# Reordering the transposes, the stores and the pooling of a pooled-attention and MLP kernel

## The chip, the core and the metric

The kernel runs on one core of a Trainium2 chip. The core has five engines that work side by side, each on its own queue of instructions in order: TensorE (PE; its weight loads are shown apart as PEld), VectorE (DVE), ScalarE (ACT), GpSimd (POOL) and SyncE (SP). SP computes nothing; it issues transfers and DMA transposes. GpSimd issues transfers too, between its own computations. The metric is the device time of the whole program in microseconds (us), as a median over runs.

## The reference

Inputs are q, k and v of shape (8 batches, 8 heads, 576 positions, 64), and two weight matrices. For each batch and head, k and v are averaged over groups of 8 neighbouring positions, so 72 pooled keys and values remain. Each of the 576 queries attends to the 72 pooled keys. The result, 4608 tokens of 512 values, goes through a two-layer block:

```python
k_p = k.reshape(B, H, Sp, pool, D).mean(axis=3)
v_p = v.reshape(B, H, Sp, pool, D).mean(axis=3)
scores = scale * np.matmul(q, k_p.transpose(0, 1, 3, 2))
attn = softmax(scores)          # written out in the reference
x = np.matmul(attn, v_p)        # then heads side by side: (4608, 512)
h = x @ w_in                    # (4608, 2048)
g = h * np.cos(h)
out = g @ w_out                 # (4608, 512)
```

## The kernel before, in words

**Two loops in one.** The MLP works on nine tiles of 512 tokens, the loop over t from 0 to 8. The attention works on eight batches of 576 tokens, and is woven into the same loop: while tile t is in the MLP, the attention of batch b = t + 1 is made. Tile t + 1 takes the last tokens of batch t and the first 448 - 64 t tokens of batch t + 1. Attention for a batch goes in chunks: u0, u1, u2 and u3 of 128 positions each, and a rest ur of 64 positions, which is made one tile later.

**One tile.** First come the up matmuls (`up_mm`, L342) with x transposed in `xT` as the moving operand. ScalarE takes a cosine of each result (L352) and VectorE multiplies (L356) into `g_sb`. Then come seven products with w_out (`down_products`, L420). Seven products take the place of eight because sums and differences of the halves of `g_sb` and of the weights are formed first: `put_g(k, i)` (L386) writes g1 to g4 from `g_sb`, each in two halves i. Some of these combinations run between the up results (at n = 3, 4 and 5), the others at the start of the products. The products use two PSUM banks in turn (A and Bb, the obanks), and after each product a VectorE read, `reads[0]` to `reads[6]` (L434, L436), takes the bank's content into SBUF. The next product in the same bank cannot start before that read. `reads[1]` frees the bank for `product(3)`. The reads write the results into `o_two`, of which there are two buffers; they are written to HBM by `rows_out` (L456), eight stores of 128 KB per tile, all issued by SP.

**The attention in a tile.** Between the products, TensorE computes scores (L222) for u0, u1 and u2, ScalarE takes the exponential (L229), and `values_rows` multiplies with the pooled v (L284). VectorE divides by the sums (`inv_rows`, L287, and `x_rows`, L289). SP then transposes `x_rows` into `xT` with a DMA transpose (L293). u3 and ur follow between the later products. The next tile's up matmuls read these columns of `xT`.

**What prepares a batch.** GpSimd loads k, q and v of the next batch (`load_kv`, L114, and `load_q`, L95) and sums groups of eight positions in `pool_add`: first sums over four pairs (L151, four instructions), then L153 (two), and for k two instructions at L156 that write `kp2`, for v one at L159 that writes `vz`. All go through one buffer `half_sums`. SP transposes pooled k into `kk` (`k_transpose`, L182) and q into `qT` (`q_transpose`, L195).

**What sets the order.** The order is written out by hand. Each engine runs its instructions in the order of the program text; waits come from the data that an instruction reads and writes. The text issues `q_transpose(b)` after the first pair of up results (n == 0) and `k_transpose(b)` after the third (n == 2), but the eight stores of the tile before stand ahead of both on SP's queue, after the transposes of u3. At the end of a tile's text GpSimd copies one element of `kk` into `gate` (L688). This copy does nothing but wait for the k transpose; the three loads of the next batch are queued behind it, and the pooling behind the loads.

Of the kernel before, what the change touches and what calls it, by code (L numbers as in the profile page):

```python
# [20 lines left out]
def kernel(  # L21
# [64 lines left out]

    staged = {}

    def even_view(src, b, j0=0, j1=KCH):
        return src[b, 2 * j0:2 * j1].rearrange("(j a) (p t) d -> (a p) j (t d)", a=2, t=ROW)
# [25 lines left out]
    def load_q(b):  # L118
        q_tile(b)
        load_even(staged["q", b], b, q)  # L120
# [21 lines left out]
            for r in range(2):  # L142
                copy(out=dst[half[r], pj0:pj1, a, 0:Sp], in_=ps[half[a]])

    def pool_add(b, which):

        st = staged.pop((which, b))
        x, s = st, half_sums
        add = nc.gpsimd.tensor_tensor
        for h in range(0, H, 2):  # L150
            add(out=s[:, h:h + 2], in0=x[:, h:h + 2, 0:4, :], in1=x[:, h:h + 2, 4:8, :], op=ADD)  # L151
        for h in range(0, H, 4):
            add(out=s[:, h:h + 4, 0:2, :], in0=s[:, h:h + 4, 0:2, :], in1=s[:, h:h + 4, 2:4, :], op=ADD)  # L153
        if which == "k":
            for slot in range(2):
                add(out=kp2[b % 2][:Sp, :, slot, :], in0=s[:, :, 0, :], in1=s[:, :, 1, :], op=ADD)  # L156
        else:
            s = s.rearrange("p (j a) t d -> p j a t d", a=2)
            add(out=v_part(b), in0=s[..., 0, :], in1=s[..., 1, :], op=ADD)  # L159
# [21 lines left out]
    def k_transpose(b):  # L181
        nc.sync.dma_start_transpose(out=kk[b % 2], in_=kp2[b % 2].rearrange("p h s d -> p (h s d)"))  # L182
# [10 lines left out]
    def q_transpose(b):  # L193
        qT_tile(b)
        nc.sync.dma_start_transpose(out=att["qT", b], in_=q_flat(b))  # L195
# [196 lines left out]
    def down_products(t):  # L392
# [36 lines left out]
        def each(out, bank, other=None, m=slice(0, HM), tk=None):  # L429

            for p in range(2) if apart else (slice(0, 2),):
                ps = bank[p] if apart else obanks[1 if bank is A else 0].rearrange("p (a m) -> p a m", a=2)
                if other is None:
                    (nc.scalar.copy if t >= B - 1 else nc.vector.tensor_copy)(out=out[:, p, m], in_=ps)  # L434
                else:
                    nc.vector.tensor_tensor(out=out[:, p, m], in0=ps, in1=other[:, p], op=ADD)  # L436
                if apart and tk is not None:
                    rows_out(t, tk, out, (p,), m, (nc.sync, nc.scalar))
# [4 lines left out]
            lambda: each(v16, A, p1),  # L443
            lambda: each(q15, Bb, p1),
            lambda: each(o2, A, q15, m2, 1),
            lambda: (each(o1, Bb, v16, m2, 0), apart or rows_out(t, 0, o1)),
            lambda: (each(o2, A, p1, m1, 1), apart or rows_out(t, 1, o2)),
        ]
        return [mms[i * 2 * HF:(i + 1) * 2 * HF] for i in range(7)], reads

    def rows_out(t, tk, o, ps=(0, 1), m=slice(0, d_model), queues=(nc.sync, nc.sync)):
        rows_of = out.rearrange("(b p t) m -> b t p m", b=B, t=ROW)
        for p in ps:
            for i, rows in enumerate(half):
                b_, pos = divmod((t * TILE + tk * HT + p * 128) // 64 + i, ROW)
                queues[i].dma_start(out=rows_of[b_, ORDER[pos], :, m], in_=o[rows, p, m])  # L456
# [93 lines left out]
    for t in range(NT):  # L550
# [5 lines left out]
        for n, fp in enumerate(up_order(t)):  # L556
            up_mm(t, fp, 2 if n < 2 else 0)
            between = ()
            if t == 0:
                if fp == 4:  # L560
                    puts = pool_k_mm(1, obanks[0], 0, 2), pool_k_mm(1, obanks[1], 2, 4)
                elif fp in (5, 6):
                    g0 = 9 * (fp - 5)
                    puts = q_transpose_mm(1, obanks[0], g0, g0 + 5), q_transpose_mm(1, obanks[1], g0 + 5, g0 + 9)
                if fp in (4, 5, 6):
                    puts[0](vec)
                    between = ((puts[1], act),)
            up_g(t, fp, between)
            if 0 < t and 3 <= n < 6:
                put_gs(*[(k, 0) for k in (((3,), (1,), ()) if t == 1 else ((1, 2), (3,), (4,)))[n - 3]])  # L570
            if 0 < t and b < B:
                if n == 0:
                    q_transpose(b)
                elif n == 2:
                    k_transpose(b)
        mms = [(ms, fc) for ms in range(4) for fc in range(FFCH)]
        if t == 0:
            mms = [(ms, fc) for hm in range(2) for cg in (0, 2, 1, 3) for ms in range(2 * hm, 2 * hm + 2)
# [36 lines left out]
        else:  # L615
# [32 lines left out]
                put_g(2, 0)  # L648
            put_gs((1, 1), (2, 1))
            reads[0]()  # L650
            put_g(3, 1)
            reads[1]()
            if t == 1:
                put_g(4, 0)
            if steady:
                values_rows(*u0)
            product(2)
            reads[2]()
            muls()
            if steady:  # L660
                values_rows(*u1)
                values_rows(*u2)
# [20 lines left out]
            reads[6]()  # L683
        if t < B:
            sin_tables()
        if 0 < t and b + 1 < B:

            nc.gpsimd.tensor_copy(out=gate, in_=kk[b % 2][0:1, 0, 0:1])  # L688
        if b + 1 < B:
            load_kv(b + 1, "k", k)  # L690
            load_q(b + 1)
            load_kv(b + 1, "v", v)
            if t == 0:
                put_weights(0, nc.gpsimd, (3, 2, 4))
                put_weights(1, nc.gpsimd, (1,))
            pool_add(b + 1, "k")
            pool_add(b + 1, "v")
# [1 line left out]
_INS = ['q', 'k', 'v', 'moe_w_in', 'moe_w_out']  # L699
_OUTS = [((4608, 512), 'float32')]  # L700
# [25 lines left out]
```

The softmax here doesn't subtract the row's maximum and nothing guards it: scores larger than these inputs give would overflow.

## Time and profile before

| What | Value |
|---|---|
| median of 3 runs | 292.55 us (292.11 to 293.8) |
| the profiled execution | 290.39 us |
| its span, first to last instruction | 288.6 us |
| TensorE matmuls busy | 275.1 us (95%) |
| VectorE busy | 217.5 us (75%) |
| ScalarE busy | 164.2 us (57%) |
| GpSimd busy | 149.7 us (52%) |
| TensorE clock granted | full in all slices |

The span is the part of the execution in which instructions of the program run. Line numbers (L342) are those of the kernel before. An answer about one stretch of the span has a line with the stretch, its length, and then busy time and number of instructions for TensorE, its weight loads, VectorE, ScalarE and GpSimd, followed by the granted clock, the mean share of the 16 DMA engines and GB/s. In a list of waits, a line says which engine and line waited, for what, how long in total, how often, and the longest. In a timeline, a line has the start, the length, the engine, the line of the kernel, the operation, output and inputs with shapes, the count, and in brackets the idle time before it and what ended that. For a DMA, the time to landing runs from its issue to the moment its data are known to have arrived.

### The profile page before, as it was taken

The numbers are of one execution on the slowest core, as the hardware profiler recorded it, in microseconds if no ns is written. First come the engines' busy times: TensorE is split into PE (matmuls) and PEld (weight loads), VectorE is DVE, ScalarE is ACT, GpSimd is POOL, SyncE is SP. The second block draws the span as 40 slices with busy tenths as digits, with TensorE's granted clock in tenths as the row PEclk, the third lists the DMA queues.
The fourth block names the chain that finished last, engine by engine and source line by source line (L and its number), as shares of the span: only waits on it lengthen the run. The fifth ranks groups of instructions, "written<-read, shape, count | busy, mean of one in ns | idle before, by whom it ended". The sixth has DMA issues, their size and how long they took to land.

```text
span 288.6 us, 5827 instructions
## 1 busy us (share of the span) xinstructions
PE 275.1 (95%) x2338; PEld 175.9 (61%) x2360; DVE 217.5 (75%) x314; ACT 164.2 (57%) x193; POOL 149.7 (52%) x145
## 2 busy tenths in 40 slices
PE   7889999999979999999799999999999999999994
PEld 2545554447854696468645884488448854884583
DVE  6458747799947995799549966996699669856972
ACT  3786798368147735773556655665557456436600
POOL 8563079996698359933995299529930000000000
PEclk9999999999999999999999999999999999999999
DMA  7999999554998699769977998699680243006014
GB/s 161 200 207 206 206 205 216 120 99 53 184 119 172 89 179 99 153 107 169 138 159 104 166 134 143 127 149 137 127 160 2 55 98 68 0 9 138 2 36 109
DMA packets 57545, 36.12 MB, mean 125 GB/s; under 512 B 35248, under 2 KB 53168, under 8 KB 57520
## 3 DMA queue, kind: packets, MB, share of 16 engines
q0 software_dynamic: 19744, 18.07, 39.9%
q1 hardware_dynamic: 37136, 17.18, 36.2%
q10 hardware_dynamic: 640, 0.52, 0.8%
q8 instruction: 18, 0.29, 0.4%
q14 instruction: 7, 0.06, 0.1%
HBM read 36.70 MB, written 9.44 MB: 160 GB/s over the span
## 4 chain that ended last, share of the span: by engine, by line
PE 61%; DVE 8%; DMA 3%; ACT 2%; issue 1%; DVEq 0%
PE obank L420 27%; PE bank L342 25%; DVE g_sb L356 4%; PE obank L342 3%; DMA xT<-x_rows 3%; PE bank L222 2%; DVE g L386 2%; PE bank L420 2%; PE bank L284 2%; ACT cos L352 1%; DVE o_two L436 1%; PE bank L257 1%; ACT ex L229 0%; DVE xT L268 0%; ACT inv L263 0%
## 5 line engine op out<-in xcount | busy, mean ns | idle before, releaser
L342 PE MATMUL bank<-xT,w_in_sb 128*128 128x512 bf16 x495 | 113.0, 379 | 4.1 <-DMA xT<-x_rows 1.6
L352 ACT ACTIVATE cos<-bank,half_pi 128x1024 f32<-128x1024 f32 x64 | 70.3, 1113 | 60.5 <-PE bank L342 59.9
L356 DVE TENSOR_TENSOR g_sb<-bank,cos 128x1024 bf16<-128x1024 f32 x64 | 77.1, 1221 | 29.2 <-ACT cos L352 29.2
L342 PEld LDWEIGHTS <-w_in_sb 128*128 128x128 bf16 x576 | 55.8, 98 | 70.1 <-DMA xT<-x_rows 3.6
L151 POOL TENSOR_TENSOR half_sums<-kv_st 72x512 f32<-72x512 bf16 x48 | 56.1, 1195 | 26.7 <-DMA kv_st<-in_k_dram 26.3
L229 ACT ACTIVATE ex<-bank 72x1024 bf16<-72x1024 f32 (+1 forms) x40 | 35.0, 928 | 34.5 <-PE bank L222 34.4
L420 PEld LDWEIGHTS <-g 128*128 128x128 bf16 x512 | 47.9, 98 | 6.1 <-issue 0.3
L420 PE MATMUL obank<-w,g 128*128 128x256 bf16 x368 | 42.6, 272 | 0.2 <-DVE p_sb L434 0.2
L420 PEld LDWEIGHTS <-g_sb 128*128 128x128 bf16 x384 | 36.6, 98 | 7.8 <-DVE g_sb L356 1.3
L153 POOL TENSOR_TENSOR half_sums<-half_sums 72x512 f32<-72x512 f32 x24 | 30.8, 1305 | 0.0
L420 PE MATMUL obank<-w_out_sb,g_sb 128*128 128x256 bf16 x240 | 29.2, 273 | 0.5 <-DVE g_sb L356 0.5
L386 DVE TENSOR_TENSOR g<-g_sb 128x1024 bf16<-128x1024 bf16 x32 | 24.3, 760 | 0.5
L289 DVE TENSOR_TENSOR x_rows<-bank,inv_rows 128x512 bf16<-128x512 f32 x24 | 16.6, 692 | 0.8
L268 DVE TENSOR_TENSOR xT<-bank,inv 64x256 bf16<-64x256 f32 x14 | 5.9, 422 | 14.6 <-ACT inv L264 14.6
L156 POOL TENSOR_TENSOR kp<-half_sums 72x512 bf16<-72x512 f32 x12 | 15.7, 1329 | 0.5
L420 PE MATMUL obank<-w_out_sb,g 128*128 128x256 bf16 x112 | 15.6, 273 | 0.0
L420 PE MATMUL obank<-w,g_sb 128*128 128x256 bf16 x128 | 15.3, 273 | 0.0
L342 PE MATMUL obank<-xT,w_in_sb 128*128 128x512 bf16 x64 | 15.1, 379 | 0.0
L359 PE MATMUL obank<-w_out_sb,g_sb 128*128 128x512 bf16 x61 | 14.7, 379 | 0.4 <-issue 0.3
L386 DVE TENSOR_TENSOR g<-g_sb,g 128x1024 bf16<-128x1024 bf16 x16 | 12.9, 809 | 0.0
L222 PE MATMUL bank<-qT,kk 64*72 64x128 bf16 (+2 forms) x288 | 12.5, 221 | 0.1
L320 ACT ACT_TABLE_LOAD x9 | 11.5, 1283 | 0.9 <-PEq L710 0.7
(102 smaller groups left out, 262.9 us busy)
## 6 DMA issues: line engine op xcount, KB each, us to landing
out_dram<-o_two SPq DMA_DIRECT2D x64, 128.0 KB, 2.4
kv_st<-in_v_dram POOLq DMA_DIRECT2D x8, 576.0 KB, 14.4
kv_st<-in_k_dram POOLq DMA_DIRECT2D x7, 576.0 KB, 7.7
q_b<-in_q_dram POOLq DMA_DIRECT2D x6, 576.0 KB, 10.2
w_in_sb<-in_moe_w_in_dram POOLq DMA_DIRECT2D x4, 512.0 KB, 13.5
w_out_sb<-in_moe_w_out_dram POOLq DMA_DIRECT2D x4, 512.0 KB, 18.3
q_b<-in_q_dram POOLq DMA_DIRECT2D x4, 288.0 KB, 12.4
g_sb<-in_k_dram SPq DMA_DIRECT2D x1, 576.0 KB, 3.5
```

The costliest lines, as they stand in the source:

```text
L151: add(out=s[:, h:h + 2], in0=x[:, h:h + 2, 0:4, :], in1=x[:, h:h + 2, 4:8, :], op=ADD)
L153: add(out=s[:, h:h + 4, 0:2, :], in0=s[:, h:h + 4, 0:2, :], in1=s[:, h:h + 4, 2:4, :], op=ADD)
L156: add(out=kp2[b % 2][:Sp, :, slot, :], in0=s[:, :, 0, :], in1=s[:, :, 1, :], op=ADD)
L222: nc.tensor.matmul(pair[:Sp, bank, c:c + n].rearrange("p (g n) -> p g n", n=64), lhsT=kk[b % 2][half[r], h0 + i, 0:Sp], rhs=att["qT", b][h ...
L229: nc.scalar.activation(out=ex[:, 0:nh * n].rearrange("p (a n) -> p a n", a=2), in_=pair[:Sp, :, 0:nh * n // 2], func=ACTF.Exp, scale=scale ...
L289: nc.vector.tensor_tensor(out=x[0:n].rearrange("p (j a d) -> p j a d", j=KCH, a=2), in0=ps[0:n, :, 0:2 * (D + 2)].rearrange("p j (a w) -> ...
L342: nc.tensor.matmul(h[j] if h is obanks else h[:, j, :], lhsT=w_in_sb[fc // 4][:, ki, (fc % 4) * 128:(fc % 4 + 1) * 128], rhs=xT[:, ki, t * ...
L352: nc.scalar.activation(out=c, in_=ps, func=ACTF.Sin, bias=half_pi[:, :1])
L356: nc.vector.tensor_mul(out=o, in0=ps, in1=c)
L359: nc.tensor.matmul(o, lhsT=g_sb[:, fc, ms * 128:(ms + 1) * 128], rhs=w_out_sb[fc // 4][:, fc % 4, :], start=(fc == 0), stop=(fc == FFCH - 1))
L386: nc.vector.tensor_tensor(out=out[:, f0:f1], in0=x, in1=y, op=op)
L420: mms.append(lambda bank=bank, first=first, g=g, w=w, fc=fc, p=p: nc.tensor.matmul(bank[p], lhsT=g(fc, p), rhs=w(fc), start=(first and fc ...
```

## The change

The change moves work on four queues, and changes no computation.

- On SP, both transposes of the batch are issued at n == 0, k before q. The eight stores of a tile are put in a list, and issued in the next tile at n == 2, after these transposes.
- The pooling is cut in two functions, `pool_first` (the four first sums) and `pool_rest`. At the end of tile t, GpSimd does k's first sums, k's rest and v's first sums. The rest of v follows in the next tile's text, at n == 2.
- The gate on `kk` and the three loads of the next batch move from the end of the text of tile t to n == 2 of the same tile, behind v's rest (in t = 1, the k load goes ahead of v's rest).
- In place of the old gate, from t = 1 on, a copy of one element of g2 holds the pooling until `put_g(2, 1)` has been written, which is between the first products.
- On VectorE, `values_rows` of u0 (the reciprocal and the division) moves ahead of `put_g(3, 1)` and of `reads[1]`. On TensorE its matmuls stand where they stood.

```diff
-    def pool_add(b, which):
-
-        st = staged.pop((which, b))
-        x, s = st, half_sums
-        add = nc.gpsimd.tensor_tensor
+    def pool_first(b, which):
+
+        x, s = staged.pop((which, b)), half_sums
         for h in range(0, H, 2):
-            add(out=s[:, h:h + 2], in0=x[:, h:h + 2, 0:4, :], in1=x[:, h:h + 2, 4:8, :], op=ADD)
+            nc.gpsimd.tensor_tensor(out=s[:, h:h + 2], in0=x[:, h:h + 2, 0:4, :], in1=x[:, h:h + 2, 4:8, :], op=ADD)
+
+    def pool_rest(b, which):
+
+        s, add = half_sums, nc.gpsimd.tensor_tensor
         for h in range(0, H, 4):
...
-            lambda: (each(o1, Bb, v16, m2, 0), apart or rows_out(t, 0, o1)),
-            lambda: (each(o2, A, p1, m1, 1), apart or rows_out(t, 1, o2)),
+            lambda: (each(o1, Bb, v16, m2, 0), apart or stores.append(lambda: rows_out(t, 0, o1))),
+            lambda: (each(o2, A, p1, m1, 1), apart or stores.append(lambda: rows_out(t, 1, o2))),
...
             if 0 < t and b < B:
                 if n == 0:
+                    k_transpose(b)
                     q_transpose(b)
                 elif n == 2:
-                    k_transpose(b)
+                    if t > 1:
+                        pool_rest(b, "v")
+                    if b + 1 < B:
+
+                        nc.gpsimd.tensor_copy(out=gate, in_=kk[b % 2][0:1, 0, 0:1])
+                        load_kv(b + 1, "k", k)
+                    if t == 1:
+                        pool_rest(b, "v")
+                    if b + 1 < B:
+                        load_q(b + 1)
+                        load_kv(b + 1, "v", v)
+            if n == 2:
+                while stores:
+                    stores.pop(0)()
...
             reads[0]()
+            if steady:
+                values_rows(*u0)
             put_g(3, 1)
             reads[1]()
             if t == 1:
                 put_g(4, 0)
-            if steady:
-                values_rows(*u0)
             product(2)
             reads[2]()
-            muls()
...
-        if 0 < t and b + 1 < B:
-
-            nc.gpsimd.tensor_copy(out=gate, in_=kk[b % 2][0:1, 0, 0:1])
         if b + 1 < B:
-            load_kv(b + 1, "k", k)
-            load_q(b + 1)
-            load_kv(b + 1, "v", v)
             if t == 0:
+                load_kv(b + 1, "k", k)
+                load_q(b + 1)
+                load_kv(b + 1, "v", v)
                 put_weights(0, nc.gpsimd, (3, 2, 4))
                 put_weights(1, nc.gpsimd, (1,))
-            pool_add(b + 1, "k")
-            pool_add(b + 1, "v")
+            else:
+
+                nc.gpsimd.tensor_copy(out=gate, in_=g2[0:1, HF - 1, 0:1])
+            pool_first(b + 1, "k")
+            pool_rest(b + 1, "k")
+            pool_first(b + 1, "v")
```

More of the change, by code (lines that the diff above doesn't have):

```diff
@@ L84 @@
     obanks = [psum.tile([128, 512], FP32, name=f"obank{i}") for i in range(2)]
-    staged = {}
+    staged, stores = {}, []
     def even_view(src, b, j0=0, j1=KCH):
```

## The prediction

> **What bounds the kernel now.** The engines' busy time comes first, then the stretches of the six tiles t = 1 to 6 (the ones that prepare another batch), cut where each tile's first up matmul starts.
>
> ```profile
> PE 275.1 (95%) x2338; PEld 175.9 (61%) x2360; DVE 217.5 (75%) x314; ACT 164.2 (57%) x193; POOL 149.7 (52%) x145
> ...
> 54.65:84.09 29.44, 27.70 (x249) 18.78 (x249) 26.25 (x36) 17.04 (x19) 24.05 (x21) 1.00 0.79 115
> 84.09:113.20 29.11, 29.00 (x254) 19.32 (x257) 22.34 (x32) 17.04 (x19) 20.51 (x20) 1.00 0.92 142
> 113.20:143.89 30.69, 29.00 (x255) 19.33 (x257) 24.95 (x37) 17.04 (x19) 20.42 (x20) 1.00 0.95 135
> 143.89:173.15 29.26, 29.02 (x255) 19.23 (x258) 22.30 (x32) 17.04 (x19) 20.41 (x20) 1.00 0.95 141
> ```
>
> TensorE (first busy column) is full: a tile without a hole takes 29.1 us. Next, who waited for whom: TensorE's idle time in these tiles is five holes, 1.46 us (t=1 to 2), 1.58 (t=3 to 4), 0.13 (t=4 to 5), and 0.25 and 0.27 inside t=5 and t=6; together 3.7 us. That is all the change can win there.
>
> ```profile
> PE bank L342 <- DMA xT<-x_rows: 1.6, 1, 1.6
> PE bank L342 <- DVE o_two L436: 1.5, 1, 1.5
> PEld L420 <- DVE g_sb L356: 1.3, 3, 0.6
> ```
>
> The second line names VectorE, but o_two was old: the weight loads of that tile wait for xT<-x_rows (1.7 us), so both big holes are late x_rows transposes. The chain of work shows the one at t=3, beside the same transposes' landing, asked of the trace for two stretches: t=3, and t=6, where nothing is loaded.
>
> ```profile
> 135.35 8.49 DMA xT<-x_rows
> 143.84 0.05 issue
> ...
> DMA to landing us min/median/max: 7.0/7.7/8.5
> ...
> DMA to landing us min/median/max: 2.5/2.5/2.5
> ```
>
> A transpose needs 2.5 us, but 7.0 to 8.5 beside the loads: in t=3 the v load lands at 143.37 (issue 128.69 plus 14.7), the first two transposes at 143.25 and 143.84. They land when the loads are over. So what is late is the load, and the GpSimd timeline says why:
>
> ```profile
> 126.96 0.18 POOL L688 COPY gate<-kk 1x1 bf16<-1x1 bf16 x1 [4.72 <-DMA kk<-kp]
> 127.08 0.85 POOL L114 DMA_DIRECT2D kv_st<-in_k_dram  x1
> 134.86 4.94 POOL L151 TENSOR_TENSOR half_sums<-kv_st 72x512 f32<-72x512 bf16 x4 [5.32 <-DMA kv_st<-in_k_dram]
> ```
>
> The gate waits 4.7 us for the k transpose, which SP issues only at 124.09, behind eight stores (6.2 us) and q's transpose (2.9). Loads start 12.3 to 13.9 us into a tile. The small holes of t=5 and t=6 have another origin: GpSimd is pooling until 8 to 10 us into the tile, and meets VectorE's first g combination.
>
> ```profile
> 182.13 1.17 DVE L386 TENSOR_TENSOR g<-g_sb 128x1024 bf16<-128x1024 bf16 x1
> 183.33 0.69 DVE L386 TENSOR_TENSOR g<-g,g_sb 128x1024 bf16<-128x1024 bf16 x1
> ```
>
> **What the Trainium skill says.** SBUF — State Buffer, "Who interferes with whom": a VectorE instruction with two SBUF inputs contends with a GpSimd instruction that reads SBUF, and the later one blocks. The trace agrees: 1.17 beside pooling, 0.69 without. DMA: Bandwidth & Descriptors, "Queues, rings and completion order": each DMA engine alternates between queues with work, packet by packet. The trace agrees in part: at t=0 four stores (128 KB) beside loads landed after 5.0 to 6.1 us against 2.4 alone, a share, not starvation; but the transposes' 7 to 8.5 us is nearly starvation. The same page, "Issuing engines are not separate DMA queues": loads, stores and transposes use the same 16 engines, so reordering them adds no bandwidth.
>
> **The change part by part.** Times are from a tile's first up matmul.
>
> *SP order.* Now: u3's x transpose (+0.3), eight stores, q, k (issued about +11). After: u3's transpose (1.2 us to issue), k (1.2; lands 2.8 after its issue, about +4.4), q (2.9; lands 4.8 after issue, +7.7), stores from +5.8 to +11. q and k are needed by the scores at +15.9: covered by 8 us. The deferred o_two buffers must be out before the next tile's second read writes o1, at +19 to +20: the first four stores are issued by +8.3 and with the 6.1 us measured beside loads land at +14.4; the others by +17 against +24. Cost nothing, with about 5 us of cover.
>
> *GpSimd order.* No instruction is added but the second gate (0.18 us, x4 or so). Pooling of one tile is 4.5 + 2.5 + 2.5 + 4.5 + 2.5 + 1.3 = 17.8 us, 18.4 with gaps. It now starts at the gate on g2 (written by +17.8), so k's kp is ready at +28, v's first sums end at +32, the rest at about +36.3, that is +7.1 of the next tile. k is landed by then (+4.4), so the loads start at about +7 where they start at +12.3 to +13.9 now. In t=1 only k starts earlier (62.5 against 67.0), q and v stay near 67.9; they then run without k ahead of them, and v lands at about 79.7 instead of 82.9.
>
> *What that does to the transposes.* From the k load's issue to u2's landing it is 16.9, 16.6 and 17.4 us now (t=1, 2, 3). The eight stores are 5.2 us of a full DMA system; they now partly run inside this stretch, but the first 3 us or so before the loads move much (after issue the loads need about 3 us to reach their rate), so I add 2 to 3. u2 lands at 7 + 17 + 3 = +27, the two before it 0.5 and 1.0 earlier; t=2 needs u2, t=3 and t=4 u1, t=5 u0, at +29.1. The holes 1.46, 1.58 and 0.13 go: **-3.17**.
>
> *Combinations without pooling.* They start at +9; pooling ends by +7.1. 0.25 and 0.27 go: **-0.52**. In t=6 that is not safe, nor in t=5 if the loads drift.
>
> *VectorE order in the products.* u0's reciprocal and x_rows (0.24 + 0.60) move ahead of put_g(3,1) and of the read that frees obank for product(3). TensorE ends u0's matmuls at 131.93 in t=3; product(3) would start at 134.01. VectorE can start u0 at 131.97 (it idles 0.4 us for it), put_g at 132.81, the read at 133.41, ending 134.10 (0.69), 0.04 to pass on: TensorE waits 0.13. But pooling now starts at +18, so put_g(3,1) at +19.6 is beside it. No row shows that one; put_g(4,1) is beside the same sums now, and took 1.10, 1.46, 1.00, 1.02, 0.86 in t=1 to 5, mean 1.09, 0.40 over its 0.69. Bounds for this put: 0 (k landed after it) to 0.77 extra. I take 0.40: a wait of 0.53 in t=2 to 5, 0.1 in t=1 (where product(3) starts 2.47 us after u0, not 2.08), 0.13 in t=6, where nothing is pooled: **+2.35**; bounds 0.65 and 3.9. The later reads shift by 0.6 us, and product(4) and (5) still find their banks free.
>
> *Stores of t=7* move behind t=8's start; t=8's o_two comes 14 us later: nothing.
>
> Sum: -3.17 - 0.52 + 2.35 = -1.34 us. The profiled execution took 290.39 (span 288.6 and 1.8 around it), which becomes 289.05. The median of the runs shown is 292.55, 2.2 above the profiled one; the difference carries over: **291.2 us**.
>
> **Rivals.**
> *Full gain.* put_g(3,1) misses the pooling, because k lands after +19.6 (7.5 us alone, up to 5 more for stores, from +7), or the read is in time. -3.69 + 0.65 = -3.0: 289.5. For it: the cost hangs on tenths. Against: k is likelier at +17.
> *The change does little: the holes stay in part.* If pooling ends at +9 and stores cost all of their 5.2 us, u2 lands at +31 in t=2: a hole of 1.9, then u1 in t=3 and t=4 at 1.0 each; the read's wait hides behind these. 3.9 - 1.71 - 1.46 + 0.2 = +0.9; half of it, with the puts still met: about 292.5, up to 293.7. For it: the DMA share is already 0.92 to 0.98 of the tile. Against: in t=3 the queues stand idle around 127 and are slow until 130.
> *Slower: starved stores.* Place: the second read, which cannot write o1 until the previous tile's first four stores have landed. Price: if they fare like the transposes and wait for the loads' end at +25, VectorE waits 5 us in each of t=2 to 5, TensorE with it: +20, less 3: about 310. It decides from a landing of +20, 12 us after issue; slower than 294.0 needs about +20.7. Against: 5.0 to 6.1 us at t=0.
> *Slower: GpSimd's own ring.* Load, pool, gate, load: if k takes 7.5 + 5.2 = 12.7 us, the ring is 31.1 us, longer than a tile; four tiles at up to 2 more, less the first hole: up to 296. It needs k to take over 10.8.
>
> **How the numbers follow.** Main case 0.45 (its own range 290.3 to 292.2), full gain 0.15, little 0.22, ring 0.11, starved stores 0.07. 0.5% is 1.46 us, about what a measurement of this kernel can tell from no change: below 291.09 lie under half of the main case, the full gain and a bit of the third: 0.40. Above 294.01: starved stores, most of the ring, the edge of the third: 0.21. Rest 0.39. Range 289.0 to 294.5; it leaves out the starved stores, half of the ring and the tail of the full gain.
>
> **What would show it.** The gate at +7 and the k transpose landed near +4.4 show the orders right; first up matmuls without a hole at t=1 to 2 and t=3 to 4, and x_rows landing at about +27, the DMA step; L386 at 0.69 in the first combinations of t=5 and 6; and a hole of 0.1 to 0.6 us before product(3), released by o_two, the cost. The prediction fails if o_two waits for a store's landing, if the loads still start after +10, or if product(3) waits over 1 us.

## The result, and the profile after

The kernel with the change takes 318.71 us (median, 318.50 to 318.97), the kernel before 292.76 us beside it (292.11 to 293.8). The ratio is 1.088, with a 95% interval of 1.085 to 1.092. The change makes the kernel 26 us slower; the forecast was 291.2 us, with a range that ended at 294.5. The profiled execution took 318.50 us, its span is 316.7 us: 28.1 us more than the profiled execution before on both counts. Ratios here and below leave out the few executions that fell into a slower state of the chip, so a ratio can differ from that of the two medians. Line numbers of the kernel after are about two higher than those of the kernel before: L422 is the line of the products, L388 that of the combinations g1 to g4, L438 that of the reads that add `p_sb`, such as those into o_two.

The engines' busy time of the kernel after, and its stretches t = 1 to 6, cut where a tile's first up matmul starts (stretch, length, busy time and instructions of TensorE, its weight loads, VectorE, ScalarE and GpSimd, then clock, DMA share, GB/s):

```profile
PE 286.2 (90%) x2360; PEld 182.0 (57%) x2360; DVE 241.2 (76%) x314; ACT 164.2 (52%) x193; POOL 152.4 (48%) x150
...
52.74:83.78 31.04, 29.44 (x257) 19.49 (x256) 28.45 (x36) 17.04 (x19) 27.76 (x25) 1.00 0.72 114
83.78:119.52 35.74, 30.40 (x259) 20.14 (x257) 28.56 (x35) 17.04 (x19) 27.42 (x27) 0.95 0.67 116
119.52:156.14 36.62, 31.28 (x259) 20.57 (x257) 29.27 (x35) 17.04 (x19) 22.01 (x21) 0.91 0.64 113
156.14:193.21 37.07, 31.73 (x259) 20.85 (x257) 29.27 (x35) 17.04 (x19) 21.31 (x21) 0.91 0.66 112
193.21:230.51 37.30, 31.96 (x259) 20.83 (x256) 29.27 (x35) 17.04 (x19) 21.10 (x20) 0.91 0.62 111
230.51:259.88 29.37, 29.11 (x259) 19.45 (x256) 23.11 (x35) 17.04 (x19) 0.00 (x0) 1.00 0.41 81
```

The prediction's stretch for t = 1 began at 54.65, 1.5 us behind that tile's first up matmul; from that matmul on, t = 1 took 30.95 us before, and takes 31.04 now. The loss sits in four tiles, t = 2 to 5, at 6 to 8 us each. In t = 6, where GpSimd has nothing left to pool, the tile is as long as before. Two columns carry it: VectorE is busy for 28.6 to 29.3 us where it needed 22.3 to 25, with the same work, and the clock falls to 0.91 on average (0.95 in t = 2).

Who waited for whom, in the kernel after (total, times, longest, in us):

```profile
POOL gate L710 <- DVE g L388: 42.1, 5, 10.7
...
PE obank L422 <- DVE o_two L438: 22.3, 6, 5.3
```

The first line is GpSimd's copy, which waits for `put_g(2, 1)` in five tiles, as intended. The waits of the up matmuls for the x_rows transposes are gone from the list. In their place TensorE waits 22.3 us for VectorE's read into o_two, six times: it is `product(3)`, which needs the bank that `reads[1]` frees. In t = 2 to 5 each wait is 5.34 us. The chain of work at the one of t = 2 (start, length, what), and the timelines of VectorE and GpSimd in the same place:

```profile
103.47 1.10 DVE g L388
104.58 4.79 issue
109.36 0.69 DVE o_two L438
```

```profile
102.87 0.69 DVE L291 TENSOR_TENSOR x_rows<-bank,inv_rows 128x512 bf16<-128x512 f32 x1
103.47 5.97 DVE L388 TENSOR_TENSOR g<-g_sb 128x1024 bf16<-128x1024 bf16 x1
109.36 0.68 DVE L438 TENSOR_TENSOR o_two<-obank,p_sb 128x512 f32<-128x512 f32 x1
```

```profile
101.82 0.18 POOL L710 COPY gate<-g 1x1 bf16<-1x1 bf16 x1 [8.00 <-DVE g L388]
101.97 4.48 POOL L149 TENSOR_TENSOR half_sums<-kv_st 72x512 f32<-72x512 bf16 x4
106.42 2.47 POOL L155 TENSOR_TENSOR half_sums<-half_sums 72x512 f32<-72x512 f32 x2
108.97 2.83 POOL L158 TENSOR_TENSOR kp<-half_sums 72x512 bf16<-72x512 f32 x2
```

`put_g(3, 1)`, 0.69 us by itself, takes 5.97 us. It comes 1.50 us after GpSimd's first add has started, in the second of six adds that follow each other without a stop. The six end at 108.89; the first add of L158 needs the result of the last one and starts only at 108.97. The combination ends at 109.44, 0.55 us after the end of the sixth add. So VectorE got nothing done between the six adds, and its turn came where GpSimd stood still for 0.08 us. `put_g(3, 1)` takes 5968 ns in each of t = 2, 3, 4 and 5, to the nanosecond. In t = 1 it met the adds 1.17 us after the first one's start, got in at the end of the second, and took 1.65 us.

The hole has a second price. Stretches around the one of t = 5 (hole 214.18 to 219.52):

```profile
216.52:218.52 2.00, 0.00 (x0) 0.00 (x0) 2.00 (x1) 0.00 (x0) 1.92 (x3) 1.00 0.14 8
218.52:219.52 1.00, 0.00 (x1) 0.00 (x0) 1.00 (x3) 0.00 (x0) 1.00 (x1) 0.53 0.00 0
219.52:224.52 5.00, 5.00 (x24) 3.48 (x24) 3.55 (x7) 0.00 (x0) 4.92 (x5) 0.50 0.27 52
224.52:225.52 1.00, 1.00 (x7) 0.69 (x6) 0.68 (x1) 0.00 (x0) 1.00 (x2) 0.56 0.00 0
225.52:230.51 4.99, 4.99 (x70) 4.22 (x68) 2.02 (x5) 3.96 (x6) 4.41 (x4) 1.00 0.00 0
```

After 4.4 us without a matmul the clock falls to half, and TensorE, busy again, goes at half speed for another 5.9 us. The work from `product(3)` to the end of the tile took 8.14 us before; behind the four holes it takes 9.42, 10.31, 10.76 and 10.99. In the trace's record of the clock the four slow stretches begin at 109.35, 143.49, 181.03 and 218.58, that is 34.14, 37.54 and 37.55 us after each other, and last 3.41, 6.83, 6.83 and 6.83 us. All are multiples of 3.41. So in this trace the clock changed only on a fixed grid of 3.41 us, and what a hole cost behind its end hung on where it fell in that grid: the four holes are equally long, but the first lost 1.28 us behind it and the last 2.85.

The sum over the span: four holes of 5.34 us, 21.4; the slow clock behind them, 1.28 + 2.17 + 2.62 + 2.85 = 8.9; new holes in t = 1, 0.74 + 0.63, and in t = 6, 0.26; less 3.2 for the transposes' holes and 0.5 for those at the combinations. That is 28.2 against 28.1 measured.

What the change was to do on the DMA side it does. GpSimd's copy that waits for `kk` and the k load of t = 2, the shortest, median and longest landing of the x_rows transposes in t = 2 to 6, and the first combinations of t = 5:

```profile
91.24 0.18 POOL L582 COPY gate<-kk 1x1 bf16<-1x1 bf16 x1
91.36 0.85 POOL L114 DMA_DIRECT2D kv_st<-in_k_dram  x1
```

```profile
DMA to landing us min/median/max: 2.4/2.5/5.5
```

```profile
202.19 0.69 DVE L388 TENSOR_TENSOR g<-g_sb 128x1024 bf16<-128x1024 bf16 x1
202.91 0.69 DVE L388 TENSOR_TENSOR g<-g,g_sb 128x1024 bf16<-128x1024 bf16 x1
```

The loads start 7.6 us into t = 2, and 4.9 to 5.4 us into the tiles after it. The transposes, once issued, land in 2.4 to 5.5 us, where those of u0 to u2 in t = 1 to 5 took 5.3 to 9.6 before, and no tile starts with a hole. The combinations of t = 5 take 0.69.

### The profile page after: what moved, and what is told of

It reads as the page before. It is cut to its first block, busy times and chain, and to the rows that moved or that the text cites. A ratio compares the mean times of both kernels' runs of the same rounds, so it can differ in the third digit from the quotient of the medians.

```text
span 316.7 us, 5848 instructions
## 1 busy us (share of the span) xinstructions
PE 286.2 (90%) x2360; PEld 182.0 (57%) x2360; DVE 241.2 (76%) x314; ACT 164.2 (52%) x193; POOL 152.4 (48%) x150
## 4 chain that ended last, share of the span: by engine, by line
PE 80%; DVE 8%; issue 8%; ACT 2%; DVEq 0%; ACTq 0%
PE bank L344 33%; PE obank L422 28%; PE obank L344 4%; PE obank L361 4%; DVE g L388 3%; PE bank L224 3%; PE bank L422 2%; DVE g_sb L358 2%; DVE o_two L438 1%; PE obank L518 1%; PE bank L259 1%; ACT cos L354 1%; ACT ex L231 1%; PE bank L286 1%; PE obank L170 1%
## 5 line engine op out<-in xcount | busy, mean ns | idle before, releaser
L422 PEld LDWEIGHTS <-g 128*128 128x128 bf16 x512 | 52.7, 106 | 33.4 <-issue 23.2
L422 PE MATMUL obank<-w,g 128*128 128x256 bf16 x368 | 51.5, 307 | 22.5 <-DVE o_two L438 22.3
L149 POOL TENSOR_TENSOR half_sums<-kv_st 72x512 f32<-72x512 bf16 x48 | 56.9, 1212 | 0.5
L388 DVE TENSOR_TENSOR g<-g_sb 128x1024 bf16<-128x1024 bf16 x32 | 46.2, 1444 | 0.5
L422 PEld LDWEIGHTS <-g_sb 128*128 128x128 bf16 x384 | 36.7, 98 | 7.7 <-DVE g_sb L358 1.0
L155 POOL TENSOR_TENSOR half_sums<-half_sums 72x512 f32<-72x512 f32 x24 | 29.8, 1260 | 0.0
L422 PE MATMUL obank<-w_out_sb,g_sb 128*128 128x256 bf16 x240 | 28.9, 273 | 0.7 <-DVE g_sb L358 0.7
L710 POOL COPY gate<-g 1x1 bf16<-1x1 bf16 x5 | 0.9, 179 | 42.1 <-DVE g L388 42.1
L158 POOL TENSOR_TENSOR kp<-half_sums 72x512 bf16<-72x512 f32 x12 | 17.4, 1467 | 0.5
L422 PE MATMUL obank<-w_out_sb,g 128*128 128x256 bf16 x112 | 15.6, 273 | 0.0
L422 PE MATMUL obank<-w,g_sb 128*128 128x256 bf16 x128 | 15.3, 273 | 0.0
L388 DVE TENSOR_TENSOR g<-g_sb,g 128x1024 bf16<-128x1024 bf16 x16 | 14.2, 889 | 0.0
```

What stands on the lines that cost most here:

```text
L149: nc.gpsimd.tensor_tensor(out=s[:, h:h + 2], in0=x[:, h:h + 2, 0:4, :], in1=x[:, h:h + 2, 4:8, :], op=ADD)
L388: nc.vector.tensor_tensor(out=out[:, f0:f1], in0=x, in1=y, op=op)
L422: mms.append(lambda bank=bank, first=first, g=g, w=w, fc=fc, p=p: nc.tensor.matmul(bank[p], lhsT=g(fc, p), rhs=w(fc), start=(first and fc ...
```

## The experiments

The theory: `put_g(3, 1)` has two inputs in SBUF, and GpSimd's adds read SBUF; one shuts the other out, and once shut out, VectorE waits not for one add but for the first stop of GpSimd, that is, the first moment in which GpSimd stands still. A combination meets a run of adds when it comes while they run; it gets in when it ends 0.55 us after the end of the add that it met. The second gate is the copy of an element of g2 (L710). Four rivals: the move of u0 alone delays the read; the loads or stores of the new order slow VectorE; the second gate alone does it; or the place in an add at which the combination comes decides. None of the kernels below leaves out an add or a combination; where an extra instruction is put in, nothing uses its result.

### One part undone, one part alone

**u0 back.** The kernel after, with `values_rows(*u0)` where it was before; everything else of the change stays. Run again beside a variant in which v's rest, in t = 1 alone, goes behind all three loads:

```diff
             reads[0]()
-            if steady:
-                values_rows(*u0)
             put_g(3, 1)
             reads[1]()
             if t == 1:
                 put_g(4, 0)
+            if steady:
+                values_rows(*u0)
             product(2)
```

> The changed kernel with u0's reciprocal and division put back behind the second read; gate, loads, stores and transposes stay as changed. Lock theory (VectorE's g combination and GpSimd's adds cannot read SBUF at once, and whether VectorE gets in at the end of an add hangs on where in the add it arrives): put_g(3,1) now arrives 0.2 us into the first add, where others (arrivals at 0.05 to 0.25 us) got in at its end, so it takes about 1.5 us, product(3) has no hole over 0.3 us, total 289 to 292. Rival 1, every combination beside pooling waits for GpSimd to run dry: put_g(3,1) still takes 6 us or more, total 315 to 325. Rival 2, the move of u0 is itself the loss: total 289 to 292 with put_g(3,1) at 0.7.

> The kernel of e1_u0_back once more, for its interval: ratio to before 0.984 to 0.990. If the first time was a chance of the two runs: 0.99 to 1.0.

Measured: 287.02 us (two executions) against 290.32, ratio 0.986 [0.980, 0.993]; again (six) 287.24 against 290.72, ratio 0.987 [0.984, 0.991]. VectorE and GpSimd in t = 2 of the kernel with u0 back:

```profile
102.12 1.46 DVE L388 TENSOR_TENSOR g<-g_sb 128x1024 bf16<-128x1024 bf16 x1
103.51 0.68 DVE L438 TENSOR_TENSOR o_two<-obank,p_sb 128x512 f32<-128x512 f32 x1
```

```profile
101.88 4.93 POOL L149 TENSOR_TENSOR half_sums<-kv_st 72x512 f32<-72x512 bf16 x4
```

The combination comes 0.24 us into the first add, gets in at its end, and takes 1.46 us; the read follows in time and no tile from t = 2 on has a hole. The four adds take 4.93 us where they took 4.48: now GpSimd waits once. One line of text moved back turns +26 us into -3.5, so loads, stores, gates and pooling of the new order do not cause the loss by themselves.

**u0 alone.** The kernel before, with only the move of u0 (the same two lines, moved forward).

> The kernel before with only u0's reciprocal and division moved ahead of put_g(3,1) and the second read. Lock theory: pooling starts after put_g(3,1) here, so it takes 0.7 us, holes of 0.1 to 0.3 us before product(3) in up to six tiles, some of it hidden in the holes at the tiles' ends: 0.3 to 1.0 us more than before (ratio 1.001 to 1.004). Rival, the move of u0 is itself the loss: 20 us more.

Measured: 292.26 us against 290.72, ratio 1.006 [1.003, 1.008]; +1.5 us, more than expected. `put_g(3, 1)` takes 0.68 to 0.69, and the x_rows holes stay (1.51, 1.76 and 0.32 us), as they should. In the profiled execution the holes of t = 1 to 6 add up to 4.3 us against 3.9 (3.7 in the prediction, which left out one of 0.23 in t = 1); the rest of the 1.5 stays unexplained. The move of u0 alone doesn't make the loss either. The two together do.

**SP alone.** The kernel before with the SP part only: k and q ahead of the stores, stores at n == 2. Pooling, gate and loads stay.

```diff
                 if n == 0:
-                    q_transpose(b)
-                elif n == 2:
                     k_transpose(b)
+                    q_transpose(b)
+            if n == 2:
+                while stores:
+                    stores.pop(0)()
```

> The kernel before with only SP's part: k and q transposes ahead of the eight stores, stores at n == 2 of the next tile. GpSimd's order stays, so the loads start when pooling ends, about 10 us into a tile in place of 12.3 to 13.9. Theory of the late loads: the hole of 1.6 us at t = 3 to 4 shrinks to 0 to 0.6, that of t = 1 to 2 stays (GpSimd is late there anyway), the small ones of t = 5 and 6 stay; 1 to 1.5 us less than before (ratio 0.995 to 0.997). If the stores beside the loads cost more than the earlier start brings: 0 to 2 us more. If stores land too late for o_two: 10 us or more.

Measured: 288.51 us (median of four, 286.65 to 291.83) against 290.72, ratio 0.989 [0.983, 0.996]. The loads start 8.9 us into t = 2 and 7.6 into t = 3, and of the transposes' holes only that of t = 1 to 2 is left (1.51). GpSimd and VectorE in t = 3:

```profile
129.91 5.48 POOL L151 TENSOR_TENSOR half_sums<-kv_st 72x512 f32<-72x512 bf16 x4 [7.11 <-DMA kv_st<-in_k_dram]
...
131.10 1.05 DVE L386 TENSOR_TENSOR g<-g_sb 128x1024 bf16<-128x1024 bf16 x1
```

The adds start here when k has landed, and by chance at `put_g(3, 1)`; it took 1.05 to 1.26 and made no hole. The medians differ by 2.2 us; the ratio makes it 3.1, with an interval of 1.3 to 4.9. So SP's order alone may bring nearly all of the 3.3 to 3.5 us that the kernel with u0 back gains, or less than half; four executions can't tell.

**SP and u0.** The same, with u0 moved forward too.

> The kernel of e10_sp_alone with u0's reciprocal and division moved ahead of put_g(3,1). As in the changed kernel, put_g(3,1) then comes 1.5 to 2.4 us after the first add starts; but here the adds start when k lands, and not behind a gate that VectorE opens. Theory that the gate's start matters: put_g(3,1) gets in at an add's end, 0.9 to 1.6 us, total 289 to 292. Theory that only the time since the first add matters (won below 1.3 us, lost above 1.5): put_g(3,1) waits until GpSimd stands still, 4.5 to 6 us in t = 2 to 5, total 308 to 319.

Measured: 293.20 us (two executions) against 290.44, ratio 1.010 [1.007, 1.013]. The new pooling and its gate are not there, and neither is a long shut-out. In t = 2 `put_g(3, 1)` came 2.5 us after the first add started, and took 0.83: later into the adds than in the kernel after, yet it got in. The loss here is made of other holes: 2.15 at t = 1 to 2 for x_rows, and 0.59, 1.27 and 0.59 before `product(2)` in t = 3 to 5, where other combinations met the adds first and the read of p_sb came late.

### The pooling moved against the combination

**The gate on g3.** The kernel after, with the second gate on what `put_g(3, 1)` writes.

```diff
-                nc.gpsimd.tensor_copy(out=gate, in_=g2[0:1, HF - 1, 0:1])
+                nc.gpsimd.tensor_copy(out=gate, in_=g3[0:1, HF - 1, 0:1])
```

> The changed kernel with the second gate on g3's last element, so that pooling waits for put_g(3,1) and not for put_g(2,1). Lock theory: put_g(3,1) takes 0.69, the hole before product(3) shrinks from 5.3 to 0.1 to 0.3 us, the clock losses after it go, total 289 to 291; put_g(4,1) then meets the adds, and if it arrives at a bad place there, 3 to 5 us per tile come back there (about 305). Rival, the move of u0 is itself the loss: total stays at 316 to 319.

Measured: 296.30 us against 290.32, ratio 1.020 [1.014, 1.025]. `put_g(3, 1)` is back at 0.68, and the loss has moved to the next combination. VectorE and GpSimd in t = 2:

```profile
107.73 4.36 DVE L388 TENSOR_TENSOR g<-g_sb,g 128x1024 bf16<-128x1024 bf16 x1
```

```profile
104.62 4.48 POOL L149 TENSOR_TENSOR half_sums<-kv_st 72x512 f32<-72x512 bf16 x4
109.06 2.48 POOL L155 TENSOR_TENSOR half_sums<-half_sums 72x512 f32<-72x512 f32 x2
111.62 2.83 POOL L158 TENSOR_TENSOR kp<-half_sums 72x512 bf16<-72x512 f32 x2
```

`put_g(4, 1)` comes in the third add and ends at 112.09, 0.55 us after the six adds: the same place on GpSimd's side, another instruction on VectorE's. TensorE waits 1.73 to 1.76 us for it in each of t = 2 to 5, and the mean clock stays at 0.998: holes of this size did not cost the clock.

**u0 back and the gate on g3.**

> The kernel of e1_u0_back with the second gate on g3's last element: put_g(3,1) meets no pooling, pooling starts about 1 us later than in e1. Only put_g(4,1) meets it, and the place decides: 0.8 to 1.5 us if it gets in at an add's end (total 286.5 to 288), or 4.4 us as in e2_gate_g3 with holes of 1.7 us in four tiles (293 to 296).

Measured: 289.64 us against 290.92, ratio 0.996 [0.994, 0.998]. `put_g(4, 1)` comes in the fourth add, takes 3.40 us in each of the four tiles, again until the stop, and leaves holes of 0.61 to 0.63.

**No second gate.** u0 back, and the pooling starts as soon as k has landed.

> The kernel of e1_u0_back without the second gate: SP's part and the earlier loads, pooling starts as soon as k lands (about 16 us into a tile in t = 2 to 5). Lock theory: pooling now meets put_g(1,1), put_g(2,1) and put_g(3,1), which stand ahead of the first reads; each can wait 0.3 us to several us, the first reads come late and product(2) or (3) waits: 292 to 315, worse than e1. If the gate is worth nothing: 286 to 288.

Measured: 295.62 us (two executions) against 290.92, ratio 1.012 [0.997, 1.026], not told from 1. In the trace three combinations in a row meet the adds (1.34, 1.53 and 1.04 us in t = 2), p_sb is read late, and `product(2)` waits 2.98, 1.25, 0.94, 1.57 and 1.02 us in t = 1 to 5. With u0 back and the gate it was 287.0 to 287.2 us, so the gate is worth having: without it no single combination is shut out for long, but more of them pay.

**A stop after the second add.** The kernel after, from t = 1 on with k's adds in the order two first sums, their second sum, two first sums, their second sum. A second sum reads what the add just before it wrote, so GpSimd stops there. The adds are the same eight, in another order.

```diff
+        for h in range(0, H, 4):
+            for i in range(h, h + 4, 2):
+                add(out=s[:, i:i + 2], in0=x[:, i:i + 2, 0:4, :], in1=x[:, i:i + 2, 4:8, :], op=ADD)
+            add(out=s[:, h:h + 4, 0:2, :], in0=s[:, h:h + 4, 0:2, :], in1=s[:, h:h + 4, 2:4, :], op=ADD)
```

> The changed kernel with k's pooling adds in another order, two first sums, their second sum, two first sums, their second sum, the same adds in all: the second sum must wait for the add just before it, so GpSimd stands still for a moment after 2.3 us and not first after 6.9 us. Theory that VectorE gets in when GpSimd stands still: put_g(3,1) ends at about 0.55 us after the second add, taking 1.3 to 1.5 us, hole 0.7 to 1.0, total 292 to 295. If standing still has nothing to do with it: put_g(3,1) keeps 6 us, total 318 to 320.

Measured: 290.99 us against 290.32, ratio 1.003 [1.000, 1.005]. GpSimd and VectorE in t = 4:

```profile
161.47 2.26 POOL L168 TENSOR_TENSOR half_sums<-kv_st 72x512 f32<-72x512 bf16 x2
163.82 1.60 POOL L169 TENSOR_TENSOR half_sums<-half_sums 72x512 f32<-72x512 f32 x1
```

```profile
162.98 1.31 DVE L398 TENSOR_TENSOR g<-g_sb 128x1024 bf16<-128x1024 bf16 x1
```

In t = 4 and 5 the combination comes 1.51 us after the first add, just where it came in the kernel after. It ends 0.55 us after the second add, at the new stop, and the next add takes 1.60 us. In t = 2 it comes 1.1 us after the first add and takes 0.68, without a wait; in t = 3 to 5 nothing is left of the loss but holes of 0.68 to 0.87. That is the test that carries the theory: the same meeting, and only the stop has moved. Only two tiles have exactly this meeting, and VectorE gets in at the end of the add that it met, as other meetings did without a stop. That it is the stop rests on two more facts: in the kernel after, the same meeting was held in all four tiles, and in all 19 waits of over 3 us in the five kernels that have them (the kernel after, two further below, and the two with the gate on g3) the combination ends 0.55 us after the add that stands before a stop.

### What decides whether it gets in

**Later by one reciprocal, and by two to six.** The kernel after, with extra reciprocals ahead of `put_g(3, 1)`: one in each tile, and in a second kernel 2, 3, 4 and 6 in t = 2, 3, 4 and 5.

```diff
                 values_rows(*u0)
+                for _ in range({2: 2, 3: 3, 4: 4, 5: 6}.get(t, 0)):
+                    nc.vector.reciprocal(out=pad, in_=u0_sums[:, :, D:D + 2])
             put_g(3, 1)
```

> The changed kernel with one more reciprocal of u0's sums (0.2 us, reads PSUM, its result is not used) ahead of put_g(3,1), so that it arrives about 0.24 us later, 0.6 us into an add. Lock theory with place of arrival: arrivals at 0.6 to 1.1 us got in at the add's end, so put_g(3,1) takes 1.0 to 1.2 us, the hole is 0.7 to 0.9 us in place of 5.3, total 292 to 295, 24 us less for one instruction more. Rival 1, waits for GpSimd to run dry whatever the place: put_g(3,1) ends at the same moment, total 318 to 320. Rival 2, the move of u0 itself: 319 to 321.

> The changed kernel with 2, 3, 4 and 6 more reciprocals of u0's sums (results not used) ahead of put_g(3,1) in t = 2, 3, 4 and 5, each about 0.12 us later by e3's trace. Lock theory with place of arrival: arrivals about 0.62, 0.74, 0.86 and 1.1 us into an add, where other combinations mostly got in at the add's end, take 0.9 to 1.3 us, holes 0.8 to 1.2; total 293 to 296. If put_g(3,1) is bound to wait for GpSimd to run dry: 5.2 to 5.8 us in all four tiles, total 318 to 321.

Measured: with one, 311.32 us in the profiled execution and 319.21 in another. The shift is only 0.12 us. In the profiled one the combination came 0.50 us into the second add in all four tiles; it was shut out in t = 2, 3 and 5 (5.85 us) and got in in t = 4 (1.20). GpSimd and VectorE in t = 3 and in t = 4:

```profile
138.43 4.48 POOL L149 TENSOR_TENSOR half_sums<-kv_st 72x512 f32<-72x512 bf16 x4
...
140.05 5.85 DVE L388 TENSOR_TENSOR g<-g_sb 128x1024 bf16<-128x1024 bf16 x1
...
175.70 4.94 POOL L149 TENSOR_TENSOR half_sums<-kv_st 72x512 f32<-72x512 bf16 x4
...
177.32 1.20 DVE L388 TENSOR_TENSOR g<-g_sb 128x1024 bf16<-128x1024 bf16 x1
```

With two to six, 319.52 us in one execution: `put_g(3, 1)` took 5.61, 5.36, 5.13 and 4.64. The later it comes, the shorter it takes, and it always ends at the stop. The place in an add does not decide: at the same place, in the same kernel, it went both ways.

**The adds later.** The kernel after, with the gate's copy made six times, so that the first add starts about 1.3 us later and the combination meets the first add.

```diff
-                nc.gpsimd.tensor_copy(out=gate, in_=g2[0:1, HF - 1, 0:1])
+                for _ in range(6):
+                    nc.gpsimd.tensor_copy(out=gate, in_=g2[0:1, HF - 1, 0:1])
```

> The changed kernel with the second gate's one-element copy made six times in a row, so that the first add starts about 1 us later and put_g(3,1) comes 0.2 to 0.8 us after it, as in e1 and e9, while VectorE's order and the rest stay as changed. Theory that the time since the first add decides behind a gate: put_g(3,1) gets in at the first add's end, 0.9 to 1.5 us, the hole before product(3) falls from 5.3 to 0.3 to 1.0 us, total 288 to 293, 26 us less for five copies more. Theory that VectorE is shut out whenever put_g(3,1) follows u0's division: 5 to 6 us as before, total 317 to 320.

Measured: 291.31 us against 290.95, ratio 1.002 [0.999, 1.004]. Five copies of one element more on GpSimd make the kernel 27 us faster. GpSimd and VectorE in t = 2:

```profile
102.38 1.36 POOL L711 COPY gate<-g 1x1 bf16<-1x1 bf16 x6 [6.78 <-DVE g L388]
103.71 4.93 POOL L149 TENSOR_TENSOR half_sums<-kv_st 72x512 f32<-72x512 bf16 x4
```

```profile
104.03 1.38 DVE L388 TENSOR_TENSOR g<-g_sb 128x1024 bf16<-128x1024 bf16 x1
```

The combination comes 0.32 us into the first add and gets in at its end; the hole before `product(3)` is 0.74 to 0.75. The last copy runs into the first add without a stop, so that a stop ahead of the first add is not what lets VectorE in. u0's division still stands just ahead of the combination, so that this order on VectorE alone is not what shuts it out.

**The gate's copy into the sums.** The second gate's copy is written into `half_sums`, which the first add overwrites, so that the first add waits for it.

```diff
-                nc.gpsimd.tensor_copy(out=gate, in_=g2[0:1, HF - 1, 0:1])
+                nc.gpsimd.tensor_copy(out=half_sums[0:1, 0, 0, 0:1], in_=g2[0:1, HF - 1, 0:1])
```

> The changed kernel with the second gate's copy written into half_sums, so that the first add waits for the gate's own end, as it would wait for k's landing; put_g(3,1) still comes about 1.4 us after the first add starts. Theory that the adds run on from the gate without a stop and that this is what shuts VectorE out: put_g(3,1) gets in at an add's end, 1.2 to 1.5 us, total 290 to 294. Theory that the time since the first add decides (below 1.3 us in, above 1.5 out): out if it comes after 1.4, total 310 to 319.

Measured: 291.25 us against 290.95, ratio 1.002 [0.999, 1.004]. The combination came 1.31 to 1.39 us after the first add's start, in the second add, and took 1.43 to 1.52; holes 0.80 to 0.89. The kernel after meets them at 1.50, so a small shift of time and the changed wait came together here, and the run can't tell which of the two let it in.

What stays open: behind the second gate, every first meeting at up to 1.39 us after the first add's start got in at the end of an add, and of those from 1.50 to 4.1 us without a stop in between, all but one (in t = 4 of the kernel with one reciprocal) were shut out until the stop. Elsewhere it is otherwise. In the kernel with SP and u0, whose adds start when k lands, `put_g(3, 1)` got in at 2.5 us. In the kernel after itself, `put_g(4, 1)` meets v's run of six adds 2.1 to 2.4 us after its start in each of t = 2 to 5, and gets in (0.75 to 1.47 us). And in t = 1 a combination that comes 0.48 us into v's rest, behind the issue of the k load, is held past the first of its two adds (2.58 us). Time since the first add alone, place in an add, kind of instruction and a stop ahead of the run are each contradicted as the one rule. What the hardware goes by, these runs don't show. That a long wait ends at the stop, they do.

### A version that is faster than both

u0 back, and in t = 1 v's rest behind the three loads:

```diff
                         load_kv(b + 1, "k", k)
-                    if t == 1:
-                        pool_rest(b, "v")
                     if b + 1 < B:
                         load_q(b + 1)
                         load_kv(b + 1, "v", v)
+                    if t == 1:
+                        pool_rest(b, "v")
```

> The kernel of e1_u0_back with v's rest in t = 1 behind all three loads, not between the k and the q load. Lock theory: the combination at 64 us no longer meets v's rest (2.5 us there, 0.65 us of it a hole of TensorE); hole gone, 0.6 us less than e1_again, the loads of t = 1 a few us earlier without effect. If the holes in t = 1 come from elsewhere: the same as e1_again within 0.2 us.

Measured: 286.15 us (six executions) against 290.72, ratio 0.984 [0.980, 0.987]; every execution of it (285.81 to 286.61) was below every one of the kernel with u0 back alone beside it (286.89 to 288.08). Its engines' busy time and two of its stretches:

```profile
PE 274.8 (97%) x2338; PEld 176.8 (62%) x2360; DVE 219.3 (77%) x314; ACT 164.5 (58%) x193; POOL 152.9 (54%) x150
...
82.83:111.78 28.95, 28.84 (x256) 19.39 (x256) 23.60 (x35) 17.06 (x19) 20.99 (x21) 1.00 0.83 143
111.78:140.73 28.95, 28.84 (x256) 19.43 (x256) 23.93 (x35) 17.07 (x19) 21.10 (x21) 1.00 0.84 143
```

All of t = 2 to 6 take 28.95 us, with no hole. In t = 1 a combination that took 2.49 us beside v's rest now takes 1.36, and its hole of 0.65 is gone. What holds it now is not settled: it comes at 64.12, GpSimd issues the v load from 64.19 to 65.03, and the first add starts only at 65.05.

## Why the prediction was wrong

**The step that failed is the bound on `put_g(3, 1)`** in the part on VectorE's order in the products. The prediction saw that this combination would meet the pooling, and that the read for `product(3)` was queued behind it. It took 0.40 us for the meeting and set the upper bound at 0.77, the worst of five rows of `put_g(4, 1)`. The meeting cost 5.28 us (5.97 less 0.69), seven times the bound. All five rows were meetings in which VectorE got in; they bounded those, not the other outcome. The prediction's own working had what was needed for a wider bound: k's first sums and the next two adds, 4.5 + 2.5 us, from which the arrival is to be subtracted. It drew on the Trainium skill, SBUF — State Buffer, "Who interferes with whom", for the rule that the later one blocks. For VectorE's two-port modes that section says that whoever issues first keeps the shared ports for the whole instruction; of a longer block it says nothing, and this is where the measurement goes further: VectorE was blocked through the second add and four more, until GpSimd stopped. Which of the two outcomes would come could not be read from the rows, and chance has a part in it: in the kernel with one more reciprocal the same meeting was held in three tiles and got in in the fourth.

**The wait's size.** Its sum was +2.35, with bounds 0.65 and 3.9; the holes before `product(3)` came to 4 x 5.34 + 0.63 + 0.26 = 22.3. The place and the releaser were right, and so was the sign to look for: the prediction said that it fails if `product(3)` waits over 1 us.

**The clock.** No step had it: 8.9 us of the 28.1. The Trainium skill, TensorE: Matmul & The Clock Gate, "What's actually happening", says that the clock falls to half after an idle window of about 3.4 us. The trace agrees in part: the clock changes on a grid of 3.41 us, and is at 0.50 from 3.0 to 4.6 us into the 5.34 us holes on. But in the kernel with one reciprocal it fell 2.13 us into the hole of t = 5 (208.28 to 213.62; the slow stretch begins at 210.41), so less than 3.4 us of idle time was enough there, while a hole of 2.98 us in the kernel without the second gate brought no fall (clock 1.00). Full speed came back after 2.7 to 5.9 us of work. For holes of the size forecast, 0.53, leaving this out would have been right: no hole of up to 2.98 us lowered the clock in these runs.

**What held.** SP's order: k's transpose landed at +4.7 to +5.2 in t = 2 to 5 (forecast +4.4). The loads: +7.6 in t = 2 as forecast (+7), and earlier still in the longer tiles. The transposes' holes, -3.17: gone, and in the kernel with u0 back, whose tiles have their usual length, gone too. So that step is right by itself, not by the delay. The combinations, -0.52: 0.69 us each in t = 5. The stores: beside loads they landed after 5.4 to 8.6 us, above the 6.1 assumed, and no read waited for them; the starved stores did not come. k's load took 9.3 to 10.9 us in these tiles, just above the 10.8 at which GpSimd's ring was said to decide, but with tiles of 36 us it had time; in the kernel with u0 back it took 9.2 to 10.2, and there is no hole either.

**What was missed in small.** In t = 1, k's load now starts ahead of v's rest, and v's rest meets the combination at n = 4: it takes 2.58 us and costs a hole of 0.74. Its end is again at a stop, behind the second of two adds. The prediction treated only the start of the loads there. And the 2.2 us by which the median shown stood above the profiled execution did not carry over: after, the median is 0.2 above, and the kernel before had medians of 290.3 to 291.0 beside the later experiments.

**The rivals.** None had this mechanism. That of the starved stores has the nearest total, about 310, but its sign, a read into o_two that waits for a store's landing, is not in the trace. The one called full gain comes close to the kernel with u0 back: that has neither the shut-out nor the late read, and took 287.0 to 287.2, 3.3 to 3.5 us less than the kernel before beside it, where the rival's sum was 3.0.

## What to carry to other kernels

When a VectorE instruction with two inputs in SBUF can meet a run of GpSimd work on SBUF, don't bound its cost by rows in which it got in: count GpSimd's run up to its next stop, and ask what is queued behind the instruction. If the two have to overlap, order GpSimd's work so that it stops often; sums that depend on the one just before did that here. To put the instruction that frees a bank ahead of the meeting should help too, but no run here tests it. A long hole in TensorE can be priced twice: behind the four holes of 5.34 us the work went at half speed for 2.7 to 5.9 us, which cost 1.3 to 2.9 us each. The clock fell as early as 2.13 us into one hole and not at all in one of 2.98, so the length alone doesn't tell.

## What the hardware showed that was not expected

- A 0.69 us VectorE instruction was held for 5968 ns, the same in four tiles, by six GpSimd adds of 1.14 to 1.25 us, and released at a stop of 0.08 us. Before that stop it let four ends of adds pass without getting in.
- When VectorE gets in, it ends about 0.55 us after an add's end, and GpSimd's next add takes 1.60 us instead of 1.14.
- The clock of TensorE went to half 3.0 to 4.6 us into holes of equal length (2.1 us into one of another run), and took 2.7 us of work to come back behind the first such hole, and 4.5, 5.4 and 5.9 behind the later ones: the changes lie on a grid of 3.41 us.
